# Small selection products fed with 112 rows, and a shorter step between attention and the first search

## The chip, the cores and the metric

The kernel runs on one core of one Trainium2 chip. The metric is the device time of one execution in microseconds (us), the median over runs. The core's engines are TensorE (PE in the profile, with its weight loads shown apart as PEld), VectorE (DVE), ScalarE (ACT) and GpSimd (POOL); SP is the queue that issues most transfers. Each engine works through its own instructions strictly in the order in which the program has them, and waits there for what another engine or a transfer has to deliver.

## The reference

Three layers one after the other, on 4 batches of 448 tokens, 12 heads of width 64 (1792 tokens, 768 features):

```python
scores = cap * np.tanh(scale * q @ k.T / cap)          # per batch and head
x = softmax(scores) @ v                                # -> 1792 x 768

logits = x @ w_gate                                    # first mixture: 8 experts
for idx in np.argsort(-logits.flatten()):              # best pair (token, expert) first
    if token_is_assigned or counts[e] >= N // E:       # each expert takes 224 tokens
        continue
    assigned[tok] = e
for e in range(8): out[mask_e] = relu(x[mask_e] @ w1[e]) @ w2[e]

y = relu(x @ w1[best]) @ w2[best] * gate               # second mixture: best expert of a token,
out = x + y                                            # where x @ w_skip > 0
```

The greedy assignment of the first mixture is what makes "searches" necessary: eight times over, the kernel finds which expert fills up next and which 224 tokens it gets.

## The kernel before

**Attention** (`attention_bounded`) works on 24 pairs of heads, in four steps for each pair, 96 steps in all. Step `n` runs the entries of the table `STEP` in order. `outs[j]` (tile `osb`) holds pair j's sums of values times probabilities, transposed, in one of 11 buffers; `sums[j]` holds the probabilities added over the parts of the keys, from which a TensorE product with ones makes the denominators. `evac` copies `outs` from PSUM. `rows1` turns a group's gate logits and denominators into rows, and `rows2` turns one pair's output into rows: four transposes on TensorE into one of two `tp` buffers, a scaling by the reciprocal (on VectorE inside the attention, as eight activations on ScalarE in the search), and one transfer into `out`. Pairs that are ready for `rows2` wait in the list `ready`; inside the attention one leaves it per four steps while it holds more than `HOLD` pairs.

**The tail** (`TAIL`) finishes pair 23: its value sums are copied, `small` makes its denominators and gate logits, `small_evac` copies those, `rows1` makes rows of them and `logits` adds them to the table `L`. For all other pairs VectorE has added up `sums`; for the last one it adds only the first two parts, and `small` multiplies the other two with ones on TensorE. `w` is one matmul whose result nobody uses, and `d` is a `rows2`.

**The first search** (`route`, p = 0) finds the first expert. It is a chain in which six digits of a threshold follow one another: VectorE compares (`r_ge`, L913), TensorE counts with 16 products (L926), VectorE tests, TensorE spreads the result over all partitions (L932). Code stops at each `yield`, a "hop"; hops 1 to 3 hold VectorE work alone, the digits begin with hop 4. `ROWS` says after which hops a `rows2` is put into the program, and what is left in `ready` comes behind the last hop. Then ranks (L970, L971) and the list of tokens follow (L986, and L994 for the token ids), the first rows are gathered, and the experts begin.

**Experts.** While the experts multiply (`mm3`: L723, L724, L725 for narrow groups, L720 and L725 for wide ones), the later searches run between the matmuls, one behind the other. A planner (`clk`, `hop`, `tick`) places its hops by fixed estimates. For p from 1 to 6 every digit ends in a product that spreads the count of passing experts, L944: the column `nok` of 8 rows, repeated 112 times, times `aboveI` (8x8). There are 36 of these. L994 makes token ids of a list, from 16 rows, two products for each of the eight lists. All 16 or 8 rows lie at partition 0.

Of the kernel before, what the change touches and what calls it, by code (L numbers as in the profile page):

```python
# [19 lines left out]
P = 112  # L20
# [7 lines left out]
def attn_moe_moe2(ctx: ExitStack, tc: tile.TileContext, q, k, v, cap, wg1, w1a, w2a, wskip, wg2, w1b, w2b, out):  # L28
# [132 lines left out]
    toid = consts.tile([16, 3], BF, name="toid")  # L161
    aboveb = consts.tile([64, P], BF, name="aboveb")
    aboveI = consts.tile([E, E], BF, name="aboveI")
# [44 lines left out]
    def constants5():  # L208
        nc.vector.tensor_tensor(eq8, identf[:16, :8], identf[:16, 8:16], op=OP.add)
        nc.vector.reduce_max(toid[:, 0:1], identf[:16, :8], axis=AX.X)  # L210
        nc.vector.reduce_max(toid[:, 1:2], identf[:16, 8:16], axis=AX.X)
        nc.vector.scalar_tensor_tensor(toid[:, 2:], toid[:, 0:1], 8.0, toid[:, 1:2], op0=OP.mult, op1=OP.add)
        nc.vector.tensor_scalar(aboveI, identf[:E, :E], ABOVE, None, op0=OP.mult)
        nc.gpsimd.memset(aboveb, ABOVE)
# [27 lines left out]
    def attention_bounded(begin, search):  # L242
# [10 lines left out]
        with tc.tile_pool(name="aw", bufs=2) as work, \  # L253
# [111 lines left out]
            def add(n):  # L365
# [36 lines left out]
            def small(j, ns):  # L402


                ps = lgt[j] = banks[j % 2]
                todo = [(slice(0, 128), sums[j][:, :1], sums[j][:, 1:])]
                todo += [(None if part(n) == 3 else slice(0, 128), prob[n][:, :1], prob[n][:, -1:]) for n in ns]
# [62 lines left out]
            HOLD = 6  # L470
# [6 lines left out]
            TAIL = 'w evac w d small sevac d w w w w rows1 logits'  # L477
            ROWS = (1, 2, 3, 5, 7, 9, 11, 13)
# [33 lines left out]
            for n in range(NS):  # L512
# [4 lines left out]
                for t in STEP:  # L517
# [16 lines left out]
                    if t == "add" and n < NS - 1:  # L534
                        add(n)
# [22 lines left out]
            steps = {"evac": lambda: evac(last, False), "small": lambda: small(last, left), "sevac": lambda: small_evac(last),  # L558
                     "rows1": lambda: (rows1([last], True), ready.append(last)), "logits": lambda: logits([last]),
                     "w": lambda: warm(1), "d": lambda: rows2(ready.pop(0)), "a": lambda: rows2(ready.pop(0), True)}  # L560
            left = [n for n in range(NS - 4, NS) if part(n) == 3 or n > [m for m in range(NS - 4, NS) if part(m) < 3][1]]
# [9 lines left out]
            while search(sum_tile):  # L571
                hops += 1
                if ready and hops in ROWS:
                    rows2(ready.pop(0), True)
            while ready:
                rows2(ready.pop(0), True)
# [65 lines left out]
    def experts_(ctx, attend):  # L642
# [202 lines left out]

        def begin():
            nc.gpsimd.memset(act, 1.0)
# [13 lines left out]
        def route():  # L861
# [23 lines left out]
            st = flat[:16, n2:n2 + T].rearrange("p (h a j) -> p h a j", h=2, j=8)  # L885
            for p in range(E):
# [14 lines left out]
                if p < E - 1:  # L901
# [4 lines left out]
                    for i, (sh, w) in enumerate(DIG):  # L906
# [27 lines left out]
                        else:  # L934
                            pc = rt([E, 64])
                            for c in range(NCH):
                                nc.tensor.matmul(pc[:, :B_], ohb[:, c, :], ge[:, c // 2, :B_, c % 2], start=(c == 0), stop=(c == NCH - 1))  # L937
                            ok = keep([E, 64], BF, "r_okt", bufs=2)
                            nok = keep([E, 1], BF, "r_nok", bufs=2)
                            nc.vector.tensor_scalar(ok[:, :B_], pc[:, :B_], float(CAP), None, op0=OP.is_ge, op1=OP.add,  # L940
                                                    accum_out=nok)
# [46 lines left out]
                nc.vector.tensor_tensor(st, bc(pl[:, :, :, None], [16, 2, P // 8, 8]), bc(eq8[:, None, None, :], [16, 2, P // 8, 8]),  # L988
# [497 lines left out]
```

## Time and profile before

| what | value |
|---|---|
| median of 3 runs (732.33 to 737.96) | 732.43 us |
| profiled execution, its own time | 734.41 us |
| its span, first to last instruction | 732.7 us |
| busy: PE, DVE, ACT, POOL | 681.3, 566.5, 429.5, 167.8 us |

The span falls into these stretches, by the busy time of the engines and the clock that TensorE was granted (1.00 is 2.4 GHz, 0.50 is 1.2 GHz):

| from, to (us) | what runs | PE busy | DVE busy | ACT busy | POOL busy | clock |
|---|---|---|---|---|---|---|
| 0 to 216.70 | attention | 212.10 | 171.96 | 185.07 | 34.55 | 1.00 |
| 216.70 to 224.85 | tail | 7.93 | 4.16 | 1.84 | 0.00 | 1.00 |
| 224.85 to 241.75 | first search | 11.42 | 9.24 | 14.85 | 0.00 | 0.63 |
| 241.75 to 255.60 | list, gather, first features | 9.78 | 6.40 | 2.12 | 4.88 | 0.71 |
| 255.60 to 490.00 | experts 0 to 4, with searches 1 to 7 | 220.30 | 197.74 | 95.41 | 77.00 | 0.98 |
| 490.00 to 732.70 | the other experts, second mixture | 219.79 | 177.00 | 130.21 | 51.41 | 0.96 |

A busy share says little about a single stretch: what counts is which engine the others wait for at its end.

### The profile page before, as it was taken

To read this page: it belongs to the slowest core of one execution; us is meant where nothing else is said; L and a number is where in the kernel's file an instruction comes from. 1 tells how busy PE (TensorE), PEld (TensorE's weight loads), DVE (VectorE), ACT (ScalarE), POOL (GpSimd) and SP (SyncE) were. 2 spreads that over 40 slices of the span, in tenths; PEclk is the share of its full clock that TensorE was granted. 3 is DMA by queue.
4 is the path that set the end of the run, shared out by engine and by line. 5 is a ranking of instruction groups with operands and counts; after the bars stand their busy time and mean duration, and the time that the engine had idled before them with its cause. 6 is when DMAs were issued, how large, how long until landed. Compare 5 with 4: busy or idle time off the path is not lost.

```text
span 732.7 us, 13921 instructions
## 1 busy us (share of the span) xinstructions
PE 681.3 (93%) x5085; PEld 530.3 (72%) x5085; DVE 566.5 (77%) x1456; ACT 429.5 (59%) x737; POOL 167.8 (23%) x207
## 2 busy tenths in 40 slices
PE   7999999999998699998999999999998999899991
PEld 4445454555445488796888887889997999889990
DVE  4888887878775489798888788797687777978781
ACT  4999898989866333342343442446663665457560
POOL 2121302111100233143332432341123021440301
PEclk9999999999997699999999999999999999999996
DMA  5543233444113755544474643748853684768701
GB/s 123 123 123 76 64 97 81 102 101 100 51 38 102 239 182 166 162 151 155 125 212 143 210 155 115 221 145 257 257 180 107 212 252 132 234 227 235 234 18 47
DMA packets 140825, 109.09 MB, mean 149 GB/s; under 512 B 53825, under 2 KB 137281, under 8 KB 140737
## 3 DMA queue, kind: packets, MB, share of 16 engines
q1 hardware_dynamic: 135408, 90.02, 41.8%
q0 software_dynamic: 4368, 17.76, 7.8%
q8 instruction: 44, 0.72, 0.4%
q14 instruction: 45, 0.36, 0.2%
q10 hardware_dynamic: 960, 0.23, 0.1%
HBM read 95.60 MB, written 13.07 MB: 148 GB/s over the span
## 4 chain that ended last, share of the span: by engine, by line
PE 67%; DVE 16%; issue 9%; DMA 3%; POOL 2%; ACT 1%; SPq 0%; POOLq 0%; DVEq 0%; ACTq 0%
PE mm L720 13%; PE mm L725 10%; PE o L363 8%; PE s L331 7%; PE mm L723 5%; PE mm L724 4%; DVE wl L697 4%; PE o L359 3%; PE rt L937 2%; PE tp L423 2%; DMA xg<-out_dram,idx 2%; PE tp L300 2%; PE s L327 2%; PE o L394 1%; PE tp L290 1%
## 5 line engine op out<-in xcount | busy, mean ns | idle before, releaser
L720 PE MATMUL mm<-h,wh 128*128 128x448 f32 x528 | 182.7, 395 | 3.4 <-DVE h L798 3.4
L690 ACT ACTIVATE wh<-raw 128x768 fp32r<-128x768 f32 (+1 forms) x158 | 145.4, 926 | 8.0 <-DMA raw<-in_moe_w_dram 8.0
L725 PE MATMUL mm<-h,wl 128*128 128x224 f32 x528 | 142.5, 270 | 2.2 <-DVE wl L697 1.5
L725 PE MATMUL mm<-x,wl 128*128 128x224 f32 x528 | 143.5, 272 | 0.7 <-DVE wl L697 0.7
L692 POOL TENSOR_TENSOR wl<-raw,wh 128x768 fp32r<-128x768 f32 (+1 forms) x33 | 72.5, 2198 | 199.6 <-ACT wh L690 167.8
L720 PEld LDWEIGHTS mm<-h,wh 128*128 128x128 f32 x528 | 102.1, 193 | 11.6 <-DVE h L798 3.9
L725 PEld LDWEIGHTS mm<-h,wl 128*128 128x128 f32 x528 | 103.7, 196 | 3.4 <-DVE wl L697 2.5
L725 PEld LDWEIGHTS mm<-x,wl 128*128 128x128 f32 x528 | 102.0, 193 | 1.1 <-DVE wl L697 1.1
L337 ACT ACTIVATE p<-s,sc 128x896 f32<-128x896 f32 x96 | 87.5, 913 | 16.4 <-PE s L331 14.5
L813 ACT ACTIVATE t<-mm 128x224 f32<-128x224 f32 x66 | 23.5, 356 | 120.8 <-PE mm L725 120.8
L723 PE MATMUL mm<-x,wh 128*128 128x224 f32 x312 | 94.0, 301 | 0.0
L697 DVE TENSOR_TENSOR wl<-raw,wh 128x256 fp32r<-128x256 f32 x199 | 91.1, 496 | 0.1
L340 ACT ACTIVATE p<-p,capc 128x896 f32<-128x896 f32 x96 | 90.4, 943 | 0.0
L703 DVE TENSOR_TENSOR wl<-raw,wh 128x768 fp32r<-128x768 f32 (+1 forms) x68 | 70.9, 1051 | 21.3 <-ACT wh L690 20.8
L724 PE MATMUL mm<-x,wh 128*128 128x224 f32 x312 | 86.7, 278 | 0.5 <-DVE x L771 0.5
L720 PE MATMUL mm<-x,wh 128*128 128x448 f32 x216 | 70.2, 381 | 0.0
L363 PE MATMUL o<-p,raw 128*64 128x448 f32 x288 | 69.8, 564 | 0.1
L331 PE MATMUL s<-sq,sk 64*128 64x448 f32 x432 | 64.7, 404 | 2.1 <-DVE sk L280 0.9
L797 ACT ACTIVATE h<-mm 128x224 fp32r<-128x224 f32 x52 | 18.6, 357 | 78.3 <-PE mm L725 77.4
L723 PEld LDWEIGHTS mm<-x,wh 128*128 128x128 f32 x312 | 60.1, 193 | 3.0 <-issue 1.1
L331 PEld LDWEIGHTS s<-sq,sk 64*128 64x128 f32 x432 | 36.0, 189 | 35.3 <-ACT p L337 13.4
L724 PEld LDWEIGHTS mm<-x,wh 128*128 128x128 f32 x312 | 60.5, 194 | 0.7 <-DVE x L771 0.7
(330 smaller groups left out, 1098.6 us busy)
## 6 DMA issues: line engine op xcount, KB each, us to landing
raw<-in_moe_w_dram SPq DMA_DIRECT2D x44, 768.0 KB, 4.9
raw<-in_moe_w_dram SPq DMA_DIRECT2D x32, 1024.0 KB, 5.5
raw<-in_q_dram SPq DMA_DIRECT2D x48, 112.0 KB, 2.9
out_dram<-xt SPq DMA_DIRECT2D x24, 224.0 KB, 2.7
raw<-in_v_dram SPq DMA_DIRECT2D x24, 192.0 KB, 2.6
raw<-in_k_dram SPq DMA_DIRECT2D x46, 96.0 KB, 2.8
raw<-in_moe_w_dram POOLq DMA_DIRECT2D x2, 768.0 KB, 7.8
raw<-in_moe_w_dram POOLq DMA_DIRECT2D x1, 1024.0 KB, 10.4
```

The source lines that it names most:

```text
L331: nc.tensor.matmul(ps[:, h, :S], kst[j][f, a, s], q[f, b], start=(m == 0), stop=(m == 2))
L337: nc.scalar.activation(prob[n], pps.pop(n)[:, :m, :S], AF.Tanh, scale=sc8)
L340: nc.scalar.activation(prob[n], prob[n], AF.Exp, scale=capc)
L363: nc.tensor.matmul(o[64 * h:64 * h + 64], v[:, s], p[:, h], start=(i == 0), stop=(i == 3), skip_group_check=True)
L690: nc.scalar.activation(wh[:, :k], src, AF.Copy)
L692: nc.gpsimd.tensor_tensor(wl[:, :k], src, wh[:, :k].bitcast(F32), op=OP.subtract)
L697: nc.vector.tensor_tensor(wl[:, a:b], src[:, a:b], wh[:, a:b].bitcast(F32), op=OP.subtract)
L703: nc.vector.tensor_tensor(wl[:, :k], src, wh[:, :k].bitcast(F32), op=OP.subtract)
L720: nc.tensor.matmul(ps.rearrange("p a t -> p (a t)"), wh[:, i, :], x[:, i].rearrange("p a t -> p (a t)"), start=first, stop=last, skip_grou ...
L723: nc.tensor.matmul(ps[:, 0], wh[:, i, :], x[:, i, 0], start=first, stop=False)
L724: nc.tensor.matmul(ps[:, 0], wh[:, i, :], x[:, i, 1], start=False, stop=False)
L725: nc.tensor.matmul(ps[:, 0], wl[:, i, :], x[:, i, 0], start=False, stop=last, skip_group_check=wide)
```

## The change

1. The two kinds of small products get 112 rows in place of 8 and 16. The added rows are zeros: `nok` becomes two fixed tiles of 112 rows and `oh` (where `st` lies) is cleared once, both by GpSimd in `begin`, in the middle of the attention; `toid` and `aboveI` are made 112 rows long, zero below.
2. VectorE adds all parts of the last pair into `sums`; `small` then has two products with ones in place of six.
3. `TAIL` loses both `d` and all but one `w`; `HOLD` goes from 6 to 3, so that three more pairs are written out inside the attention; `osb` has 8 buffers, not 11; the search writes out 8 pairs, two of them after hop 1, the last after hop 11; before it wrote out 9, the last two of them after hop 13 and behind the last hop.

```diff
-    toid = consts.tile([16, 3], BF, name="toid")
+    toid = consts.tile([P, 3], BF, name="toid")
-    aboveI = consts.tile([E, E], BF, name="aboveI")
+    aboveI = consts.tile([P, E], BF, name="aboveI")
...
-                if n == full[2] and j < NH // 2 - 1:
+                if n == full[2]:
                     ADD[1].tensor_tensor(s, s, prob[n], op=OP.add)
-                if n == max(full[1], xs[0]) and j < NH // 2 - 1:
+                if n == max(full[1], xs[0]):
...
-                outs[j] = work.tile([128, S], F32, name="osb", bufs=11)
+                outs[j] = work.tile([128, S], F32, name="osb", bufs=8)
...
-                for i, (k, *x) in enumerate(todo):
-                    for h in range(2):
-                        kk = k or slice(64 * h, 64 * h + 64)
-                        nc.tensor.matmul(ps[64 + 32 * h:96 + 32 * h], ones[kk], x[h][kk, 0], start=(i == 0), stop=(i == len(ns)),
-                                         skip_group_check=True)
+                for h in range(2):
+                    nc.tensor.matmul(ps[64 + 32 * h:96 + 32 * h], ones, sums[j][:, h], start=True, stop=True, skip_group_check=True)
...
-            HOLD = 6
+            HOLD = 3
...
-            TAIL = 'w evac w d small sevac d w w w w rows1 logits'
-            ROWS = (1, 2, 3, 5, 7, 9, 11, 13)
+            TAIL = 'evac small sevac w rows1 logits'
+            ROWS = (1, 1, 2, 3, 5, 7, 9, 11)
...
+            for t in noks:
+                nc.gpsimd.memset(t, 0.0)
+            nc.gpsimd.memset(oh, 0.0)
...
-            st = flat[:16, n2:n2 + T].rearrange("p (h a j) -> p h a j", h=2, j=8)
+            st = flat[:, n2:n2 + T].rearrange("p (h a j) -> p h a j", h=2, j=8)
...
-                            nok = keep([E, 1], BF, "r_nok", bufs=2)
+                            nok = noks[i % 2]
...
-                            nc.tensor.matmul(pn, bc(nok, [E, P]), aboveI, start=True, stop=True)
+                            nc.tensor.matmul(pn, bc(nok, [P, P]), aboveI, start=True, stop=True)
```

From the first expert on every engine's order is the same in both kernels. The first of the two places where it differs most is TensorE from the tail to the first digit; `lgs` are the gate logits and denominators, `thr` the unused matmul, `r_ge` the first digit's comparison. Before:

```order
L423 MATMUL tp<-identf,osb 112x128 x4
L411 MATMUL o_197<-sums,ones 32x448 x2
L411 MATMUL o_197<-p,ones 32x448 x4
L413 MATMUL o_197<-osb,raw_71 32x448
L423 MATMUL tp<-identf,osb 112x128 x4
L131 LDWEIGHTS thr
L131 MATMUL s<-thr 112x448
```

After (its L406, L407 and L417 are before's L411, L413 and L423):

```order
L417 MATMUL tp<-identf,lgs 112x96 x4
L406 MATMUL o_199<-sums,ones 32x448 x2
L407 MATMUL o_199<-osb,raw_71 32x448
L131 LDWEIGHTS thr
L131 MATMUL s<-thr 112x448
L417 MATMUL tp<-identf,lgs 112x128 x4
L417 MATMUL tp<-identf,osb 112x128 x16
L924 LDWEIGHTS r_ge_2557
```

Four products of `p` and both `rows2` of the tail are gone, and four `rows2` (16 transposes) now stand ahead of the first digit's count, where before there were three.

The other place is VectorE at the last pair's sums (`sums`, `p`), the split of its probabilities (`px`) and the last `rows2` of the attention (`xt`). Before:

```order
L372 TENSOR_TENSOR sums<-p 128x896
L348 CAST px<-p 128x448
L349 TENSOR_TENSOR px<-p,px 128x448
L450 TENSOR_TENSOR xt<-tp,rec 112x512
L433 RECIPROCAL rec<-tp 112x4x6
L435 TENSOR_TENSOR g<-tp,rec 112x4x48
```

After (L444 is before's L450, L427 its L433):

```order
L372 TENSOR_TENSOR sums<-p 128x896
L375 TENSOR_TENSOR sums<-sums,p 128x896
L348 CAST px<-p 128x448
L349 TENSOR_TENSOR px<-p,px 128x448
L444 TENSOR_TENSOR xt<-tp,rec 112x512
L379 TENSOR_TENSOR sums<-sums,p 64x448 x2
L427 RECIPROCAL rec<-tp 112x4x6
```

One addition now stands ahead of the split, and two behind the `xt` of a `rows2`.

## Rows read from the trace of the kernel before

**Rows 1.** Timeline of PE round one L944: start us, duration us, engine, line.

```profile
260.65 0.27 PE L725 MATMUL mm<-x,wl 128*128 128x224 f32 x1
260.85 0.21 PE L944 MATMUL rt<-aboveI,r_nok 8*112 8x8 bf16 x1
260.99 0.37 PE L723 MATMUL mm<-x,wh 128*128 128x224 f32 x1
261.19 0.28 PE L724 MATMUL mm<-x,wh 128*128 128x224 f32 x1
```

**Rows 2.** Timeline of PE round L970 and L971, two products of 112 rows.

```profile
279.51 0.27 PE L725 MATMUL mm<-x,wl 128*128 128x224 f32 x1
279.62 0.18 PE L970 MATMUL rt<-r_cum,onesb 112*112 112x32 bf16 x1
...
279.70 0.35 PE L723 MATMUL mm<-x,wh 128*128 128x224 f32 x1
279.89 0.28 PE L724 MATMUL mm<-x,wh 128*128 128x224 f32 x1
```

**Rows 3.** Timeline of PE, the id products of one list.

```profile
363.04 0.26 PE L994 MATMUL rt<-toid,oh 16*112 16x3 bf16 x2
```

**Rows 4.** The chain that ended last, first and last L944 on it: start, us.

```profile
260.92 0.15 PE rt L944
...
469.38 0.14 PE rt L944
```

**Rows 5.** Timeline of DVE, copies of `outs` of pairs 4, 5, 8 and 9.

```profile
57.44 0.61 DVE L384 COPY osb<-o 128x448 f32<-128x448 f32 x1
65.16 0.61 DVE L384 COPY osb<-o 128x448 f32<-128x448 f32 x1
...
91.09 0.61 DVE L384 COPY osb<-o 128x448 f32<-128x448 f32 x1
99.38 0.62 DVE L384 COPY osb<-o 128x448 f32<-128x448 f32 x1
```

**Rows 6.** Timeline of all engines, end of the attention and tail.

```profile
209.69 1.26 DVE L379 TENSOR_TENSOR sums<-sums,p 64x448 f32<-64x448 f32 x2
...
215.41 0.93 PE L394 MATMUL o<-sums,ones 128*32 128x448 f32 x6
...
216.96 0.69 DVE L450 TENSOR_TENSOR xt<-tp,rec 112x512 f32<-112x512 f32 x1 [2.01 <-PE tp L423]
...
221.11 0.94 PE L413 MATMUL o<-osb,raw 128*32 128x448 f32 x2
...
222.43 0.54 ACT L417 ACTIVATE lgs<-o 128x448 f32<-128x448 f32 x1 [4.32 <-PE o L413]
...
224.85 0.29 DVE L889 TENSOR_REDUCE r_m<-L 112x16 f32<-112x128 f32 x1
```

**Rows 7.** Timeline of all engines, the first search's beginning and its end.

```profile
225.72 3.62 ACT L448 ACTIVATE xt<-tp,rec 112x64 f32<-112x64 f32 x17
...
226.13 0.65 PE L423 MATMUL tp<-identf,osb 128*112 128x128 f32 x4 [1.00 <-ACT xt L448]
...
227.25 0.67 PE L926 MATMUL s<-r_ohb,r_ge 112*64 112x8 bf16 x16 [0.47 <-DVE r_ge L913]
...
239.95 0.23 DVE L966 TENSOR_TENSOR_SCAN r_cum<-onesb,r_aq 112x32 bf16<-112x32 bf16 x1
...
241.75 0.18 PE L970 MATMUL rt<-r_cum,onesb 112*112 112x32 bf16 x1 [1.88 <-ACT xt L448]
```

**Rows 8.** Windows: PE, PEld, DVE, ACT, POOL busy us (x instructions), clock, DMA share, GB/s.

```profile
224.85:241.75 16.90, 11.42 (x133) 8.92 (x132) 9.24 (x50) 14.85 (x70) 0.00 (x0) 0.63 0.42 119
...
255.60:490.00 234.40, 220.30 (x2078) 195.94 (x2077) 197.74 (x708) 95.41 (x172) 77.00 (x63) 0.98 0.52 164
```

**Rows 9.** Timeline of PE after a long wait of expert 1.

```profile
341.24 0.55 PE L937 MATMUL rt<-r_ge,r_ohb 112*8 112x32 bf16 x16 [2.89 <-DVE r_ge L913]
...
342.37 0.60 PE L720 MATMUL mm<-h,wh 128*128 128x448 f32 x1
...
345.17 0.41 PE L720 MATMUL mm<-h,wh 128*128 128x448 f32 x1
```

More of the change, by code (lines that the diff above doesn't have):

```diff
@@ L400, in gates_of, with small @@
                                      skip_group_check=True)
-            def small(j, ns):
+            def small(j):
                 ps = lgt[j] = banks[j % 2]
-                todo = [(slice(0, 128), sums[j][:, :1], sums[j][:, 1:])]
-                todo += [(None if part(n) == 3 else slice(0, 128), prob[n][:, :1], prob[n][:, -1:]) for n in ns]
-                for i, (k, *x) in enumerate(todo):
-                    for h in range(2):
-                        kk = k or slice(64 * h, 64 * h + 64)
-                        nc.tensor.matmul(ps[64 + 32 * h:96 + 32 * h], ones[kk], x[h][kk, 0], start=(i == 0), stop=(i == len(ns)),
-                                         skip_group_check=True)
+                for h in range(2):
+                    nc.tensor.matmul(ps[64 + 32 * h:96 + 32 * h], ones, sums[j][:, h], start=True, stop=True, skip_group_check=True)
                 nc.tensor.matmul(ps[:32], wgb[:, j % NP], outs[j], start=True, stop=True, skip_group_check=True)
@@ L533, in attention_bounded @@
                         split_p(n + SA)
-                    if t == "add" and n < NS - 1:
+                    if t == "add":
                         add(n)
@@ L557, in attention_bounded @@
                 events.pop((t, n))()
-            steps = {"evac": lambda: evac(last, False), "small": lambda: small(last, left), "sevac": lambda: small_evac(last),
+            steps = {"evac": lambda: evac(last, False), "small": lambda: small(last), "sevac": lambda: small_evac(last),
                      "rows1": lambda: (rows1([last], True), ready.append(last)), "logits": lambda: logits([last]),
                      "w": lambda: warm(1), "d": lambda: rows2(ready.pop(0)), "a": lambda: rows2(ready.pop(0), True)}
-            left = [n for n in range(NS - 4, NS) if part(n) == 3 or n > [m for m in range(NS - 4, NS) if part(m) < 3][1]]
             for t in TAIL.split():
@@ L572, in attention_bounded @@
                 hops += 1
-                if ready and hops in ROWS:
+                for _ in range(min(len(ready), ROWS.count(hops))):
                     rows2(ready.pop(0), True)
-            while ready:
-                rows2(ready.pop(0), True)
+            assert not ready
     def attention_any(begin, search):
@@ L844, in experts_ @@
         dma = keep([P, ND, NCH], I32, "dma")
+        noks = [keep([P, 1], BF, "r_nok%d" % i) for i in range(2)]
         def begin():
+            for t in noks:
+                nc.gpsimd.memset(t, 0.0)
+            nc.gpsimd.memset(oh, 0.0)
             nc.gpsimd.memset(act, 1.0)
@@ L938, in route @@
                             ok = keep([E, 64], BF, "r_okt", bufs=2)
-                            nok = keep([E, 1], BF, "r_nok", bufs=2)
+                            nok = noks[i % 2]
                             nc.vector.tensor_scalar(ok[:, :B_], pc[:, :B_], float(CAP), None, op0=OP.is_ge, op1=OP.add,
-                                                    accum_out=nok)
+                                                    accum_out=nok[:E])
                             yield 0.5, 0.3
                             pn = rt([P, E])
-                            nc.tensor.matmul(pn, bc(nok, [E, P]), aboveI, start=True, stop=True)
+                            nc.tensor.matmul(pn, bc(nok, [P, P]), aboveI, start=True, stop=True)
                             n = keep([P, 1], F32, "r_n", bufs=2)
```

8 lines of the change are left out of this document (4 added, 4 removed).

## The prediction

> **What bounds the kernel now.** I read the stretches first. In the longest one that the change touches, the experts with the later searches, TensorE is busy 220.3 of 234.4 us and VectorE 197.7 [rows 8]: TensorE leads, with only 14 us of idle time, and VectorE has 37. Then the chain that ended last, in the same stretch, for the small products themselves: 32 of the 36 L944 stand on it, the first and the last of these in [rows 4], and 6 of the 7 L994 pairs that fall there (one pair is the first search's, before 255.6). So what one of them takes of TensorE is on the path. Of the 32, 28 are reached along TensorE and 4 from VectorE. Last, the timeline of the stretch from the last attention step to the first expert, where every step waits for one before it and no engine is full: the first search takes 16.9 us, at a mean granted clock of 0.63 [rows 8].
>
> **The products of 112 rows.** In [rows 1] one product of 8 rows stands between an L725 and an L723; from L725 to the next L724, whose starts the product and the two transitions move, it is 260.65 to 261.19, 0.54 us. In [rows 2] two products of 112 rows and 112 columns stand in the same place: 279.51 to 279.89, 0.38 us, for one product more. So at least 0.16 is saved if the 8-row product becomes a 112-row one. From L970 to L723 it is 0.08 for the two, 0.04 each; one less gives 0.34, so 0.20 is saved. I take 0.20. The L994 pair, 16 rows [rows 3], has the same forms of transition ahead and behind, and I give it 0.20 too.
>
> On the path: 28 x 0.20 = 5.6 for the L944 reached along TensorE; 4 x 0.10 = 0.4 for those reached from VectorE, where only the transition behind the product can shrink; 6 x 0.20 = 1.2 for L994. Together 7.2. Not all of it stays: each stretch of TensorE on the chain ends where VectorE waits for a search value, and if TensorE gets there earlier, VectorE is soon the later one. VectorE's 37 us of idle time are spread over those places, five times what is to be saved, so I let four fifths through: **-5.8**. Ends: -7.2 if all goes through, 0 if the rows are not what makes the product dear.
>
> What [rows 1 and 2] show is a transition: 0.20 us from L725 to the 8-row product, 0.11 from L725 to the 112-row one. The Trainium skill, TensorEngine Tiling (Array Packing), Key Properties, says that changing the tiling mode drains TensorE; the two spacings agree. The page TensorE: Matmul & The Clock Gate, LDWEIGHTS (loading the stationary operand), speaks against the edit: a load takes as long for 32 rows as for 128, only columns count. By that alone the product gains nothing from fewer or more rows, and the sum would be without this term; it is the first rival below.
>
> The clearing of `oh` and `nok` is GpSimd's, in the middle of the attention, beside 34.55 us of its work in 216.7 (table of the stretches); I cost it at nothing. If GpSimd were late with its split of v behind it, a step would wait for at most that clearing.
>
> **Three more pairs inside the attention.** They come into the 6th, 12th and 13th group of four steps. [Rows 5] give the price: the 6th group has no `rows2` and takes 65.16 - 57.44 = 7.72; the 10th, the same kind of group, has one and takes 99.38 - 91.09 = 8.29. So 0.57 each, TensorE's transposes nearly in full, and three make **+1.7**. Their transfers go into SP's queue ahead of loads for a unit several groups later, which hides them; the 8 buffers of `osb` are each free two steps before they are written again, by the order of steps.
>
> **The tail.** Before, the search's first instruction L889 starts at 224.85 [rows 6]. After, VectorE's `xt` of the attention's last pair ends at 216.96 + 0.69 = 217.65, and the two additions that now stand behind it take 1.26 (as at 209.69): `sums` is whole at 218.91. The addition ahead of the split falls on a VectorE that has little to do there, idle 2.01 ahead of that `xt`, and I cost it at nothing; without that cover it would cost about what the two behind take, 1.26. Then two products with ones and the one for the gate, in three column groups, like the three of L394 that took 0.93 together: 219.85. From the copy `lgs` to L889 it was 224.85 - 222.43 = 2.42, and nothing in that changes: 222.3. The tail ends **-2.5** earlier. If the gate product ran behind the two instead of beside them, it would cost its 0.94 [rows 6] more, so the ends are -2.5 and -1.6.
>
> **The first search.** With T for the start of L889: ScalarE takes 3.62 / 17 x 8 = 1.70 per pair [rows 7]. Only two `tp` buffers exist, so the third pair's transposes waited for ScalarE and came at T + 1.28 (226.13); the first count at T + 2.40 (227.25) was hidden from it. Now a fourth pair stands ahead of the count. Its buffer comes free 1.70 later, at T + 2.98, its transposes take 0.65, and TensorE, in order, counts at T + 3.6: **+1.2**. At half clock the transposes and the count take nearly twice as long, which adds up to 0.8; the mean of 0.63 says that the clock is down for most of this search already, and with five unused matmuls gone it may be down from its start. I take +1.6, between +1.2 and +2.0. The later pairs come into gaps that VectorE's compares leave, as before.
>
> At the end the ranks' L970 waited 1.88 for ScalarE's last pair and began at 241.75, while its input L966 was done at 239.95 + 0.23 [rows 7]. No pair is left there now, so up to 241.75 - 240.25 = 1.5 goes: **-1.4**. What is late next is VectorE's chain of digits itself. The weights' first loads stand behind the same pair in SP's queue and get no later; what an earlier start of theirs does to the gather I don't price.
>
> **The sum.** +1.7 - 2.5 + 1.6 - 1.4 = -0.6 up to the first expert, -5.8 after it: -6.4. The profiled execution took 734.41 for a span of 732.7, 1.7 more outside it, and would come to 728.0. It is 2.0 above the median of the three runs, so I go from the median: 732.43 - 6.4 = 726.0. A change of 1%, 7.3 us, is about what a measurement of this kernel can tell from none.
>
> **Rivals.**
> 1. The rows don't matter: the 8-row product is dear for its place among wide matmuls of another type, or for its one broadcast column. For it: [rows 2] differ from [rows 1] in the moving width too. Against it: the spacing ahead of the product, 0.20 against 0.11, has passed before anything moves through it. The time is 732.43 - 0.6 = 731.8. Chance 0.12.
> 2. VectorE takes the saving: its compares and splits become the later part at most places, and only a quarter of the 7.2 is left. For it: VectorE is busy 84% of the stretch, and TensorE's longest wait there, 2.89, is for a compare [rows 9]. Then -1.8 - 0.6: 730.0. Chance 0.15.
> 3. Everything goes through, and the earlier end of output rows lets the first gather land earlier as well: -7.2, -0.6 and up to 1 more: 723.6. Chance 0.15.
> 4. Slower: the clock. After TensorE's wait of 2.89 the wide matmul takes 0.60 against 0.41 at 345.17 [rows 9], so from 341.7 to 345.2 the clock is at its lower level, and of those 3.4 us nearly half is lost, 1.6. A TensorE that reaches VectorE's values sooner waits longer; each further wait that brings the clock down costs 1.6. The gain of 6.4 is gone from four more on, and with nine in the seven searches it would be 732.43 - 6.4 + 14.4 = 740. What speaks against it: most waits there are far under 2.89. The page TensorE: Matmul & The Clock Gate, HAM oscillation, tells of a kernel that falls back to the lower clock at its gaps between matmuls; [rows 9] agree, and by that rule alone this rival would be likelier than I make it. Chance 0.06.
>
> **How the numbers follow.** The forecast, 726.0, has 0.52. Its own range is 723 to 729: the share that goes through from a half to all (3.6 to 7.2), the tail and the search by 0.9 and 0.4 either way. Cases 1 and 2 reach to 731.8, case 3 down to 722.5. The range 722 to 732 leaves out the slower case and a little at either end. Faster by over 1% is under 725.1: a third of the forecast's 0.52 and all of case 3, 0.33 to 0.36. Slower by over 1% is case 4 alone.
>
> **What would show it.** In the profile after: L725 to L942 (the new number of L944) at 0.11 and L725 to L724 round it at 0.34, not 0.54; attention's last copies 1.7 later; the search's first instruction 0.8 earlier; the first count 3.6 to 4.4 behind it, with transposes released by ScalarE just ahead; no wait of the ranks' product for ScalarE; about the same or a longer wait of TensorE for VectorE among the experts, and the granted clock there still 0.98. The forecast is wrong if the spacing stays at 0.54, if the experts' stretch shrinks by less than half of 7.2 though the spacing has shrunk, or if the clock there falls.

## The result and the profile after

The changed kernel takes 725.28 us (median of 4 runs, 723.87 to 725.78); the kernel before, beside it on the same chip, 733.2 (4 runs, 732.33 to 737.96). The ratio is 0.9876, interval 0.983 to 0.9921: it is faster, by 7.9 us between the medians, by 9.1 by the ratio, and by the interval at least 5.8. The forecast was 726.0, 6.4 less than before. The profiled execution took 725.78 for a span of 724.0; of before it was 734.41 and 732.7. The ratios here leave out runs more than 1.5% above their kernel's fastest, so they need not be the quotient of the medians.

First the products. The changed kernel's timeline of PE (start us, duration us, engine, line, operation), round one spreading product, which is now L942; L717 is what was L725:

```profile
274.45 0.28 PE L717 MATMUL mm<-x,wl 128*128 128x224 f32 x1
274.56 0.17 PE L942 MATMUL rt<-aboveI,r_nok 112*112 112x8 bf16 x1
274.60 0.35 PE L715 MATMUL mm<-x,wh 128*128 128x224 f32 x1
274.78 0.27 PE L716 MATMUL mm<-x,wh 128*128 128x224 f32 x1
```

From L717 to the product it is 0.11, from L717 to L716 0.33; in [rows 1] the same steps were 0.20 and 0.54. That holds for all of them: over the 20 products that stand among matmuls of this size and wait for nothing the median goes from 0.55 to 0.33, over the dozen among wide ones (448 columns) from 0.64 to 0.42. The pairs of id products, whose price was taken over by likeness, save the same: from L717 to L716 round a pair among the same matmuls it is 0.38 or 0.39, before it was 0.60. So 0.22 is saved at each, where the forecast had 0.20.

Second the tail. All engines at the end of the attention; these rows answer to [rows 6], and L406, L407, L411, L444 and L887 are what was L411, L413, L417, L450 and L889:

```profile
219.23 0.69 DVE L444 TENSOR_TENSOR xt<-tp,rec 112x512 f32<-112x512 f32 x1 [1.59 <-PE tp L417]
...
219.83 1.26 DVE L379 TENSOR_TENSOR sums<-sums,p 64x448 f32<-64x448 f32 x2
...
220.59 1.12 PE L406 MATMUL o<-sums,ones 128*32 128x448 f32 x3 [0.46 <-DVE sums L379]
...
221.16 0.56 PE L407 MATMUL o<-osb,raw 128*32 128x448 f32 x1
...
222.51 0.54 ACT L411 ACTIVATE lgs<-o 128x448 f32<-128x448 f32 x1 [2.13 <-PE o L407]
...
224.74 0.29 DVE L887 TENSOR_REDUCE r_m<-L 112x16 f32<-112x128 f32 x1
```

The two additions (1.26) stand behind `xt`, the gate product L407 runs beside the sums L406, and from `xt` to the search's first instruction it is 224.74 - 219.23 = 5.51, before 224.85 - 216.96 = 7.89: 2.38 saved.

Third the first search, the same view; these rows answer to [rows 7] (L442, L417, L924, L964 and L968 were L448, L423, L926, L966 and L970):

```profile
226.02 0.65 PE L417 MATMUL tp<-identf,osb 128*112 128x128 f32 x4 [1.00 <-ACT xt L442]
...
227.66 0.65 PE L417 MATMUL tp<-identf,osb 128*112 128x128 f32 x4 [0.99 <-ACT xt L442]
...
228.24 1.00 PE L924 MATMUL s<-r_ohb,r_ge 112*64 112x8 bf16 x16
...
240.98 0.22 DVE L964 TENSOR_TENSOR_SCAN r_cum<-onesb,r_aq 112x32 bf16<-112x32 bf16 x1
...
241.26 0.27 PE L968 MATMUL rt<-r_cum,onesb 112*112 112x32 bf16 x1 [1.40 <-DVE r_cum L964]
```

A fourth pair's transposes (227.66), released by ScalarE, stand right ahead of the first count, which is 3.50 behind the search's first instruction (before 2.40). It takes 1.00, before 0.67, since the clock fell at 228.3; in the second profile of this kernel it falls 5.5 behind the search's first instruction and not 3.6, and the count takes 0.67 there too. The ranks' product waits for VectorE's `r_cum`, and no longer for ScalarE.

Fourth the two long stretches, as windows (PE, PEld, DVE, ACT, POOL busy us with instructions, clock, DMA share, GB/s); they answer to [rows 8]:

```profile
224.74:241.26 16.52, 10.79 (x129) 8.44 (x128) 9.33 (x50) 13.00 (x63) 0.00 (x0) 0.61 0.39 112
253.60:478.23 224.63, 207.62 (x2067) 189.35 (x2068) 195.17 (x702) 94.98 (x172) 77.18 (x61) 0.99 0.55 172
```

The second window goes from the first expert matmul to the write of the eighth list's ids. Between the same two events before had 488.38 - 255.58 = 232.80 us, with TensorE busy 218.70. So the stretch is 8.2 us shorter, TensorE has 11.1 less to do in it, and it waits 2.9 more (17.0 against 14.1).

All kernels below are read by the same five events of their timelines, in us of their own span: the copy of `outs` of pair 22, the search's first instruction, the ranks' product, the first expert matmul, the eighth list's ids. The last column is the distance of the last two.

| kernel | pair 22 | search | ranks | experts | list 8 | experts to list 8 |
|---|---|---|---|---|---|---|
| before | 210.98 | 224.85 | 241.75 | 255.58 | 488.38 | 232.80 |
| after | 213.25 | 224.74 | 241.26 | 253.60 | 478.23 | 224.63 |
| after, second profile (after_again) | 212.72 | 224.23 | 240.42 | 253.71 | 480.05 | 226.34 |
| e1_products | 210.88 | 224.74 | 241.65 | 255.68 | 482.12 | 226.44 |
| e2_tail | 212.98 | 224.48 | 240.67 | 253.58 | 489.13 | 235.55 |
| e3_clear224 | 212.87 | 224.37 | 240.58 | 253.65 | 479.77 | 226.12 |
| e4_rows13 | 213.18 | 224.67 | 239.86 | 252.86 | 480.15 | 227.29 |
| e5_rowcount | 213.43 | 224.92 | 241.13 | 254.22 | 480.95 | 226.73 |
| e6_best | 212.93 | 224.43 | 239.88 | 252.91 | 477.54 | 224.63 |
| e7_best_warm | 213.81 | 225.29 | 240.62 | 254.03 | 477.09 | 223.06 |
| e8_weights_late | 213.77 | 225.26 | 241.74 | 254.05 | 475.40 | 221.35 |
| e9_weights_behind | 213.33 | 224.83 | 241.23 | 260.09 | 482.05 | 221.96 |
| e10_rows14 | 213.44 | 224.94 | 242.87 | 257.23 | 479.79 | 222.56 |

### The profile page after: what moved, and what is told of

It is laid out like the page before. It is cut to its first block, busy times and chain, and to the rows that moved or that the text cites. A ratio compares the mean times of both kernels' runs of the same rounds, so it can differ in the third digit from the quotient of the medians.

```text
span 724.0 us, 13895 instructions
## 1 busy us (share of the span) xinstructions
PE 667.9 (92%) x5072; PEld 524.4 (72%) x5072; DVE 568.0 (78%) x1460; ACT 427.6 (59%) x729; POOL 171.2 (24%) x210
## 4 chain that ended last, share of the span: by engine, by line
PE 66%; DVE 16%; issue 10%; DMA 3%; POOL 2%; ACT 1%; SPq 0%; POOLq 0%; DVEq 0%; ACTq 0%
PE mm L712 13%; PE mm L717 9%; PE o L363 8%; PE s L331 7%; PE mm L715 4%; PE mm L716 3%; DVE wl L689 3%; PE o L359 2%; PE tp L417 2%; DMA xg<-out_dram,idx 2%; PE rt L935 2%; PE tp L300 2%; PE s L327 2%; PE o L394 1%; PE tp L290 1%
## 5 line engine op out<-in xcount | busy, mean ns | idle before, releaser
L717 PE MATMUL mm<-h,wl 128*128 128x224 f32 x528 | 142.6, 270 | 3.9 <-DVE wl L689 2.0
L717 PE MATMUL mm<-x,wl 128*128 128x224 f32 x528 | 142.6, 270 | 0.5 <-DVE wl L689 0.5
L717 PEld LDWEIGHTS mm<-h,wl 128*128 128x128 f32 x528 | 103.7, 196 | 5.5 <-DVE wl L689 3.3
L717 PEld LDWEIGHTS mm<-x,wl 128*128 128x128 f32 x528 | 101.1, 191 | 0.7 <-DVE wl L689 0.7
L715 PE MATMUL mm<-x,wh 128*128 128x224 f32 x312 | 92.9, 298 | 0.0
L689 DVE TENSOR_TENSOR wl<-raw,wh 128x256 fp32r<-128x256 f32 x199 | 88.3, 482 | 0.1
L716 PE MATMUL mm<-x,wh 128*128 128x224 f32 x312 | 85.9, 275 | 0.3 <-DVE x L763 0.3
L716 PEld LDWEIGHTS mm<-x,wh 128*128 128x128 f32 x312 | 59.8, 192 | 0.5 <-DVE x L763 0.5
```

What stands on the lines that cost most here:

```text
L689: nc.vector.tensor_tensor(wl[:, a:b], src[:, a:b], wh[:, a:b].bitcast(F32), op=OP.subtract)
L715: nc.tensor.matmul(ps[:, 0], wh[:, i, :], x[:, i, 0], start=first, stop=False)
L716: nc.tensor.matmul(ps[:, 0], wh[:, i, :], x[:, i, 1], start=False, stop=False)
L717: nc.tensor.matmul(ps[:, 0], wl[:, i, :], x[:, i, 0], start=False, stop=last, skip_group_check=wide)
```

## The experiments

The theory is that of the prediction: the small products are dear because few rows divide TensorE's array in another way than the 128-row matmuls round them, and most of what they save stays. Its rivals are that the rows don't matter, that VectorE takes the saving, and that the gain comes from the tail and the earlier output rows.

**The two halves apart.** e1_products is the kernel before with the products and the clearing alone (cut to the main lines):

```diff
                             pn = rt([P, E])
-                            nc.tensor.matmul(pn, bc(nok, [E, P]), aboveI, start=True, stop=True)
+                            nc.tensor.matmul(pn, bc(nok, [P, P]), aboveI, start=True, stop=True)
...
+            nc.gpsimd.memset(oh, 0.0)
```

> The kernel before with the products of 112 rows and the clearing alone; attention, tail and first search as before. Theory (changing the array's rows costs, and most of it is on the path): 0.33 from the matmul ahead of the spreading product to the second one behind it, as after, against 0.55; the searches among the experts end 5 to 6 us sooner; the clearing costs 0.8 in the attention; the first expert begins 0.8 later than before: 733.2 - 5.5 + 0.8 = 728.5. Rival (the gain of the whole change came from the shorter start and from fewer spells at the lower clock): the spacing shrinks, but VectorE takes it: 732 to 733.

Measured: 728.36 (12 runs, 722.2 to 733.73) against 732.46 (23 runs), ratio 0.9917, 0.9888 to 0.9946: 6.1 us less, 4.0 to 8.2. e2_tail is the rest alone (cut to two lines of it):

```diff
-            TAIL = 'w evac w d small sevac d w w w w rows1 logits'
-            ROWS = (1, 2, 3, 5, 7, 9, 11, 13)
+            TAIL = 'evac small sevac w rows1 logits'
+            ROWS = (1, 1, 2, 3, 5, 7, 9, 11)
```

> The other half alone: tail, sums, output rows and 8 buffers as after, products of 8 and 16 rows, no clearing. Theory: attention 1.7 longer, tail 2.4 shorter, first count 1.1 later, no wait for ScalarE ahead of the ranks; the ranks begin about 1.3 sooner than before, and because output rows no longer stand ahead of the weights in the queue, the first expert's first matmul comes 2.8 sooner: 733.2 - 2.8 = 730.4. Rival (the early gather of the profile after was chance): the first matmul comes 1.3 sooner, 731.9.

Measured: 731.66 (12 runs, 727.21 to 735.98) against 732.46, ratio 0.9991, 0.9958 to 1.0025. The first expert matmul comes 2.0 sooner than before, where 2.8 was expected. The two windows of the expert stretch, e1_products first and then e2_tail:

```profile
255.68:482.12 226.44, 212.91 (x2069) 194.51 (x2068) 194.57 (x703) 95.27 (x172) 76.70 (x61) 0.96 0.53 168
```

```profile
253.58:489.13 235.55, 220.65 (x2067) 196.19 (x2066) 196.10 (x703) 95.16 (x172) 76.76 (x61) 0.96 0.51 163
```

With the products alone, TensorE's busy time falls from 218.70 to 212.91, by 5.8, and the stretch by 6.4, though the granted clock there is lower than before; with the tail alone the eighth list comes 0.75 later than before. The measured gain is the products'. The rest is no loss and no gain that these times can tell.

The profiles tell more if they are read from list to list (each time the write of a list's ids, as in the last event above). Each entry is the length in us, with the granted clock:

| lists | before | e2_tail | after | e9_weights_behind |
|---|---|---|---|---|
| 2 to 3 | 36.36, 1.00 | 36.75, 0.96 | 35.45, 1.00 | 35.43, 1.00 |
| 3 to 4 | 40.69, 0.96 | 41.43, 0.92 | 39.77, 0.96 | 37.00, 1.00 |
| 4 to 5 | 36.21, 1.00 | 36.22, 1.00 | 35.26, 1.00 | 35.69, 1.00 |
| 5 to 6 | 36.71, 1.00 | 36.72, 1.00 | 35.50, 1.00 | 35.49, 1.00 |
| 6 to 7 | 39.66, 0.96 | 41.50, 0.92 | 36.63, 1.00 | 36.64, 1.00 |
| 7 to 8 | 12.46, 1.00 | 12.45, 1.00 | 12.61, 1.00 | 12.60, 1.00 |

The first of these as windows, of before and of after:

```profile
286.29:322.65 36.36, 34.96 (x338) 30.79 (x336) 30.11 (x113) 14.05 (x27) 11.10 (x8) 1.00 0.48 152
```

```profile
283.01:318.46 35.45, 34.03 (x338) 30.46 (x337) 30.17 (x113) 14.18 (x28) 11.12 (x8) 1.00 0.51 158
```

Two things follow. An interval holds six spreading products and one pair of id products, 7 x 0.22 = 1.54 us of spacing saved. In the three intervals that have the full clock before and after (2 to 3, 4 to 5, 5 to 6) the saving is 0.91, 0.95 and 1.21: two thirds of it stay. And e2_tail, which is 2.23 ahead of before at its second list (284.06 against 286.29), falls back by 2.97 in just the three intervals in which its clock is lower than before's; in the other three both agree to 0.01. So the earlier start of the experts is passed on as far as the clock is the same, and this one profile lost it to the clock.

**How many rows it takes.** e5_rowcount gives the spreading products of one search different rows (the values of `nok` all stand in the first 8, the others are zero):

```diff
-                            nc.tensor.matmul(pn, bc(nok, [P, P]), aboveI, start=True, stop=True)
+                            rn = (16, 32, 64, 96, 112, 112)[i]
+                            nc.tensor.matmul(pn, bc(nok[:rn], [rn, P]), aboveI[:rn], start=True, stop=True)
```

> After, with the spreading product of the six digits fed with 16, 32, 64, 96, 112 and 112 rows (the other rows are zeros in every case, so the values are those of after). From the matmul ahead to the second one behind it, plain spacing being 0.22 among narrow matmuls. Theory (what costs is a change of how the array's rows are divided): 16 and 32 rows 0.55 as before's 8, 96 and 112 rows 0.33; 64 rows, the half, 0.55 too. Rival (the cost falls with the rows used): a step from each to the next, 64 rows about 0.45. Second rival (any number under 112 is dear): 96 rows 0.55.

Its timeline of PE, round a product of 64 rows and one of 96 (the spreading product is L943 here):

```profile
266.72 0.27 PE L717 MATMUL mm<-x,wl 128*128 128x224 f32 x1
266.93 0.21 PE L943 MATMUL rt<-aboveI,r_nok 64*112 64x8 bf16 x1
267.06 0.37 PE L715 MATMUL mm<-x,wh 128*128 128x224 f32 x1
267.27 0.27 PE L716 MATMUL mm<-x,wh 128*128 128x224 f32 x1
...
269.06 0.28 PE L717 MATMUL mm<-x,wl 128*128 128x224 f32 x1
269.18 0.17 PE L943 MATMUL rt<-aboveI,r_nok 96*112 96x8 bf16 x1
269.21 0.35 PE L715 MATMUL mm<-x,wh 128*128 128x224 f32 x1
269.40 0.27 PE L716 MATMUL mm<-x,wh 128*128 128x224 f32 x1
```

From L717 to L716 it is 0.55 with 64 rows and 0.34 with 96. The medians by rows: 16, 32 and 64 all have 0.55, 96 has 0.335 and 112 has 0.33. So it is a step between 64 and 96 rows, not a slope. Neighbours, type, columns and the one broadcast column are the same in all five, which leaves nothing of the rival by which the rows don't matter, nor of those by which the cost falls evenly or any number under 112 is dear. (One run, 726.53; its time tells nothing more.)

**The clearing.** GpSimd's clearing of `oh` was costed at nothing. e3_clear224 clears the 224 columns of each row that the id product reads, instead of 1792:

```diff
-            nc.gpsimd.memset(oh, 0.0)
+            nc.gpsimd.memset(oh.rearrange("p a c -> p (a c)")[:, NCH * (T // 8 + 24):NCH * (T // 8 + 24) + T], 0.0)
```

> After, with GpSimd clearing only the 224 columns of oh that st uses, not 1792. Theory (the long clearing holds VectorE's copy up, and through it TensorE): the copy that took 0.94 in the eighth group takes 0.39 again, that group loses its extra 0.8, and the time is 725.3 - 0.8 = 724.5. Rival (that group is longer for another reason, such as the first use of the eighth osb buffer): the group keeps its 0.8 and the time stays at 725.3.

Measured: 724.08 (6 runs), ratio 0.986, 0.9814 to 0.9905, not to be told from the change as it was. But the place shows it. After, all engines in the 8th group of four steps:

```profile
76.88 1.58 POOL L844 MEMSET oh<- 112x1792 bf16 x1
...
78.55 0.39 POOL L846 COPY avail<-desc 112x8 f32<-112x8 f32 x1
78.81 0.94 DVE L348 CAST px<-p 128x448 fp32r<-128x448 f32 x1
...
79.80 0.47 PE L359 MATMUL o<-px,vx 128*128 128x448 f32 x1 [1.00 <-DVE px L348]
```

and with the small clearing:

```profile
77.06 0.28 POOL L844 MEMSET oh<- 112x224 bf16 x1
...
79.00 0.39 DVE L348 CAST px<-p 128x448 fp32r<-128x448 f32 x1
79.44 0.68 PE L359 MATMUL o<-px,vx 128*128 128x448 f32 x2 [0.45 <-DVE px L348]
```

In these two VectorE's copy to `px` takes 0.94 where GpSimd's copy and clearings run beside it, and 0.39 where they are over; TensorE waits 1.00 for it, or 0.45, and in the kernel before 0.21. It isn't so in every execution. In after_again, the second profile of the changed kernel, the copy takes 0.39 at the same place, and GpSimd's next clearings are the ones that take longer:

```profile
78.85 0.39 DVE L348 CAST px<-p 128x448 fp32r<-128x448 f32 x1
78.92 0.36 POOL L848 MEMSET dsh<- 112x16 int32 x1
```

In the seven profiles that have the moved row and the long clearing this group is 0.50 to 1.01 longer than before (0.79 in after, 0.50 in after_again); in the four that have the moved row without it (e2_tail has no clearing; e3_clear224, e6_best and e7_best_warm have the small one) it is 0.24 to 0.30. In e1_products, which has the long clearing but not the moved row, the copy takes 0.39 and the group is no longer than before (+0.01, where its expectation had 0.8). So 0.24 to 0.30 goes with the moved row, and another 0.2 to 0.8, by the execution, with the long clearing that has become its neighbour.

**Where the rows of the first search go.** e4_rows13 gives its eight pairs the hops of the kernel before, one pair to a hop:

```diff
-            ROWS = (1, 1, 2, 3, 5, 7, 9, 11)
+            ROWS = (1, 2, 3, 5, 7, 9, 11, 13)
```

> After, with the output rows of the search after hops 1, 2, 3, 5, 7, 9, 11, 13, one per hop. Theory (the fourth pair ahead of the first count is what made it late; the last pair after hop 13 is done before the ranks need the bank): first count 2.4 behind the search's first instruction, not 3.5; ranks 1.1 sooner, the first matmul of the experts too: 725.3 - 1.1 = 724.2. Rival (the gather and the first weights came early only because the last output rows were written two digits before them): the ranks come 1.1 sooner, but the weights' load waits for the last rows again and the gather takes over 6 to land, 726.

Measured: 723.39 (6 runs), ratio 0.9859, 0.9816 to 0.9903. Its first count is 2.40 behind the search's first instruction again, and from there to the ranks it is 239.86 - 224.67 = 15.19 us, after 16.52. Part of these 1.33 is the clock, which falls 3.6 us behind the search's first instruction in after and 5.1 behind it here. Between profiles that are nearer in this it is 1.00 (after_again, where the clock falls after 5.5 and the ranks come after 16.19) and 1.07 (after against e6_best, which has the rows of e4_rows13, a fall after 3.1, and 15.45). So the second pair of the first hop costs 1.0 to 1.1, which is what the first count shows, and a pair at hop 13 brings no wait of the ranks. The first expert matmul comes only 0.74 sooner than after, since the gathers take 5.5 us to land, after 4.6: of the rival, the longer landing came, though not its 726. e10_rows14 puts the last one at hop 14 instead, `ROWS = (1, 1, 2, 3, 5, 7, 9, 14)`, to bring back the wait that the change took away.

> After, with the last output rows of the search moved from hop 11 to hop 14, where the kernel before had its last ones. Theory (the start is earlier because no output rows stand ahead of the ranks' bank and of the weights in SP's queue): the ranks wait for ScalarE again, 1 us or more, the weights are issued 1 to 2 later, the gather lands in over 5.5, and the first matmul of the experts comes 2 later than in after; time 727. Rival (the start of the first expert is set by the digits alone): under 0.5 later.

```profile
242.87 0.19 PE L968 MATMUL rt<-r_cum,onesb 112*112 112x32 bf16 x1 [1.71 <-ACT xt L442]
```

In this timeline the ranks' product waits for ScalarE again, and comes 242.87 - 224.94 = 17.93 behind the search's first instruction, 1.41 more than after and 1.74 more than after_again; the forecast had 1.4 for this. The first expert matmul comes 3.63 later than after, where 2 was expected. The time is 726.34 (5 runs), ratio 0.9908, 0.9865 to 0.9952.

**The gather and the weights.** After, the first expert matmul comes 1.98 sooner, though the ranks come only 0.49 sooner. The two gathers of the first list's rows land 4.6 us after their issue (median), before 6.4. e8_weights_late was to issue the two loads of weights on SP's queue behind the gather's:

```diff
-        hop_until(won, 0)
-        pump(2)
         hop_until(listed, 0)
         busy0(24)
         fetch_rows(0)
+        pump(2)
```

> After, with the first two loads of weights put behind the first gather in the program. Theory (the gather landed 2 us sooner after the change because the weights started 1.3 sooner and were less in its way): with the weights behind it the gather lands in 4.6 us or less, the first split waits for its weights instead, and the first expert begins 2 to 4 later. Rival (the gather came sooner because the output rows were written long before): its landing stays at 4.6 whatever the weights do.

It did not act: SP, with nothing else queued, issued them at 242.32, 0.58 behind the ranks, as after (241.84, also 0.58). So its 723.5 (4 runs, ratio 0.9847, 0.9801 to 0.9893) is one more time of the change itself. e9_weights_behind gives all five loads to GpSimd's queue, where they stand behind the gather, by leaving `pump(2)` out.

> After, with all five first loads of weights issued by GpSimd behind its two gathers, so that none is on its way when the gather starts (in the run before with the same aim the queue issued them at the same time as in after, so it told nothing). Theory (weights in the gather's way set its landing): the gather lands in under 4.4, the weights land 4 to 6 later than in after, and the first split, not the gather, ends the start last. Rival (output rows in the gather's way): landing stays at 4.4 to 4.8.

The gathers land after 4.4, hardly sooner than after, but the weights come late and the experts start at 260.09 (728.37, one run). In e10_rows14, with a late output row and the weights issued at 244.28, the gathers take 6.9. The issues of both stretches, e10_rows14 first and then after (median us from issue to landing):

```profile
raw<-in_moe_w_dram SPq DMA_DIRECT2D x2, 768.0 KB, 5.7
...
xg<-out_dram,idx_all POOLq DMA_INDIRECT x2, 6.9
```

```profile
raw<-in_moe_w_dram SPq DMA_DIRECT2D x2, 768.0 KB, 6.0
...
xg<-out_dram,idx_all POOLq DMA_INDIRECT x2, 4.6
```

So where the last output row and the weights come earlier, the gather lands 2 us sooner. In all profiles the landing goes with the time by which the weights are issued ahead of the first gather: 4.4 to 4.5 us ahead it lands after 4.5 to 4.7 (after, after_again, e2, e3, e5, e8), 4.1 ahead after 5.1 to 5.6 (e4, e6, e7), 3.5 to 3.6 ahead after 6.4 to 6.9 (before, e1, e10), and with the weights behind it after 4.4 (e9). The last output row, which lands 2.7 us after its issue (median), should by this estimate be over even in e10_rows14 (242.84 + 2.7 = 245.5; the gather is issued at 247.81). That speaks for the weights. It isn't shown, because the row was moved along with them in every kernel but e9_weights_behind.

**The best of these, and the clock.** e6_best has the small clearing and the rows of e4_rows13. e7_best_warm adds the five unused matmuls that the change took out of the tail, `TAIL = 'w evac w small sevac w w w w rows1 logits'`, to see if they hold the clock in the first search. after_again is the changed kernel, unaltered, on the same chip.

> After with both edits that were tried one by one: GpSimd clears 224 columns of oh, and the search's output rows come after hops 1, 2, 3, 5, 7, 9, 11, 13. Theory (the two are at different places and add up): the eighth group 0.4 shorter, the ranks 1.1 sooner and with them the first matmul of the experts: 1.3 to 1.6 less than after. Rival (the start is soon lost again in the experts): the first matmul comes sooner, and the time is that of after.

> The same with all the unused matmuls of the kernel before put back into the tail, six in place of one. Theory (they keep the clock up into the first search, but cost TensorE time only where it waits): the clock falls one or two us later, the first counts take 0.67 in place of 1.0, the ranks come 0.3 to 0.5 sooner. Rival (they stand in TensorE's order ahead of the last pair's sums and transposes): the search's first instruction comes 0.4 later and nothing is won.

> After once more, for a second profile of the same program and a narrower interval. Theory (executions of one program differ by the spells of TensorE's lower clock in the experts, 1.6 to 1.9 us for each that falls where TensorE leads): up to the first expert every time agrees within 0.4 with the first profile, and further on the two drift apart only across such spells. Rival (they differ all along, by transfers): the difference grows evenly.

| kernel | us | runs | ratio to before | interval |
|---|---|---|---|---|
| e6_best | 723.01 | 6 | 0.9846 | 0.9807 to 0.9885 |
| e7_best_warm | 724.35 | 6 | 0.9858 | 0.982 to 0.9896 |
| after_again | 724.68 | 6 | 0.9842 | 0.9799 to 0.9886 |

e6_best reaches its ranks 15.45 behind the search's first instruction, after_again 16.19, but no time here separates the three. With the unused matmuls the clock falls at 230.2 instead of 227.5, 4.9 behind the search's first instruction instead of 3.1; but the changed kernel alone shows 3.6 and 5.5 in its two profiles, so this isn't shown to be their doing. The ranks come 15.33 behind the first instruction instead of 15.45: nothing is won.

The expectation for after_again held in its second half. Up to the first expert the two profiles of one program differ by more than the 0.4 that it allowed, by 0.84 at the ranks: 0.29 of it arises in the group with the clearing, 0.33 in the first search, where the clock falls later, and the rest at the start. Among the experts they agree to 0.15 from list to list where both have the full clock, and differ by 0.49 and 0.81 from list 3 to 4 and from 6 to 7, where the clock differs.

One thing about the clock goes with how the experts begin. The first 12 us of the experts as windows, of before, e1_products, after and e6_best in this order:

```profile
255.58:267.58 12.00, 10.99 (x106) 9.73 (x104) 10.97 (x32) 5.26 (x11) 4.14 (x2) 0.86 0.66 217
```

```profile
255.68:267.68 12.00, 11.52 (x82) 10.72 (x81) 9.17 (x26) 4.79 (x9) 4.14 (x2) 0.57 0.65 215
```

```profile
253.60:265.60 12.00, 9.48 (x108) 8.60 (x109) 11.01 (x34) 5.72 (x11) 4.10 (x2) 1.00 0.78 262
```

```profile
252.91:264.91 12.00, 9.33 (x109) 8.46 (x108) 11.01 (x35) 5.68 (x11) 4.15 (x2) 1.00 0.70 235
```

Where TensorE waited 0.88 to 1.67 us for the gathered rows behind its unused matmuls (before 1.23, e1_products 1.67, e4_rows13 0.88, e10_rows14 1.40) the clock drops to its lower level at the start of the experts, to a mean of 0.57 to 0.86; in the eight profiles where it waited for the first of them 0.35 or not at all it is 1.00 throughout. In e9_weights_behind, where TensorE waited 6.79 a little later, the experts begin at the lower level too. With one short drop the stretch up to the second list costs little more (29.47 in e4_rows13, 29.56 in e6_best), since VectorE is busy 11.0 of the 12 us and sets the pace; with the long drop of e1_products it is 31.48.

## Why the prediction was right

The sign, the range and the main term held: 725.28 against 726.0. That the number came so near is in part luck: the attention cost more than was forecast, while the first search's fourth pair cost less and the gather gave a gain that was not priced. By its own steps:

- **The products, -5.8.** Right in mechanism and near in size. The spacing saved is 0.22 where 0.20 was taken, and the products alone save 6.1 us by their ratio (4.0 to 8.2) and 5.8 of TensorE's busy time. e5_rowcount shows that it is the rows. The Trainium skill, TensorEngine Tiling (Array Packing), Key Properties, has a change of tiling mode drain TensorE; the step between 64 and 96 rows agrees. No view here shows the drain itself. The share of four fifths was too high and the base too small, and the two errors cancel: six intervals between lists save 6 x 1.54 = 9.2 us of spacing, where the forecast counted 7.2 for the products on the chain, and two thirds of that stay by the three intervals at full clock, 6.1. What is lost shows as waits of TensorE, 17.0 us in the stretch after, 14.1 before.
- **Three more rows in the attention, +1.7.** Mis-sized. The 6th, 12th and 13th groups grew by 0.57, 0.57 and 0.58, as forecast. The 8th, for which nothing was forecast, grew by 0.79: about 0.25 with the moved row, the rest with the clearing costed at nothing (0.50 in all in the second profile). Together 2.5, of which 2.27 shows at pair 22, since this profile reaches the attention's pairs 0.27 sooner from the start.
- **The tail, -2.5.** Right: 2.38, with the gate product beside the sums. (The row of L394 that it was likened to holds six products, not three; the time came out all the same.) With the longer attention, the search begins 0.1 sooner and not 0.8, in the second profile 0.6.
- **The fourth pair, +1.6.** Right in mechanism, mis-sized. The fourth pair's transposes and the first count came 2.92 and 3.50 behind the search's first instruction, forecast 2.98 and 3.6 at full clock: 1.10 later than before, and e4_rows13 prices the pair at 1.0 to 1.1 over the whole search. The addition for half clock did not come, as the clock was still full while these transposes ran (0.65). Nor is it "nearly twice": at the lower level four transposes take 1.10 for 0.65 and a count 1.02 for 0.67. **The ranks' wait, -1.4**, went as said, and e10_rows14 brings it back at 1.4 to 1.7. The ranks come 0.49 sooner than before, in the second profile 1.33, forecast 0.6.
- **Gather and weights, not priced.** They gave another 1.5: the experts start 1.98 sooner. In the profiles this start is passed on where the clock is the same. e2_tail loses its own only where its clock is lower; e9_weights_behind, whose experts start 6.5 later than after's, has its second list 6.19 later, and comes within 3.8 at the eighth because after's clock is lower from list 3 to 4 (39.77 against 37.00). The time of e2_tail, 3.1 less to 1.8 more, holds the whole 2.0 and nothing.
- **The clock.** The rival that feared it did not come: the granted clock of the expert stretch is 0.99 after and 0.98 before. Single profiles of kernels with the new products go from 0.95 to 1.00 there, but over all runs on record the mean clock of a whole execution is 0.960 to 0.964 before, by the group of runs, and 0.962 to 0.967 with them. Three stretches of it in before (from 256.5, 341.5, as in [rows 9], and 444) run the same matmuls in 0.41 for 0.27 or 0.60 for 0.41; the first profile of after has one, from 337.5. That accounts for some 2 us of the 8.2 by which its stretch is shorter: from list 6 to 7, where only before has one, 3.03 are saved, elsewhere some 1. It is not the change's doing: the second profile of the same kernel has three, and a stretch shorter by 6.5.
- **VectorE takes the saving** (730.0). Refuted by the ratio of e1_products, whose interval ends at 4.0 us less; 1.8 would be a quarter. VectorE's `r_ge` is waited for 6.8 us in five places after, 5.9 in four before: the waits grow, as said, but little.

What stays open: the halves, 6.1 and 0.7 by their ratios, make 6.8, and the whole, as it was timed with its near copies, 0.984 to 0.988, some 9 to 12. The intervals are wide enough to meet. Read from the profiles at equal clock the halves make more, 6.1 from the lists and 2.0 from the start. Part may be the clock at the start of the experts, which is full only where the early gather is, and which in e1_products cost 1.9 us (31.48 against 29.56); this was read from single profiles and not tried by itself.

## What to carry to other kernels

A small matmul between large ones costs what it does to its neighbours, so read the spacing from the matmul ahead to the second one behind, not its own duration; if its rows are few and the others have 128, filling it up with zero rows can be worth more than the rows cost. An edit on an idle engine is not free if it can hold up the engine beside it: look at what it will stand beside after all other edits, not at its place before. And compare two profiles stretch by stretch, where both have the same clock, before you call a gain lost or won: two profiles of one program differed here by 1.8 us at the eighth list.

## What had not been expected of the hardware

- The cost of a product of few rows is a step: 0.55 us of spacing for 16, 32 and 64 rows, 0.33 for 96 and 112.
- VectorE's copy of 128x448 took 0.93 to 1.22 instead of 0.39 beside GpSimd's work; in e1_products and after_again it took 0.39 and GpSimd's clearings of 112x16 beside it up to 0.36 instead of 0.11. The Trainium skill, SBUF — State Buffer, Who interferes with whom, has GpSimd and a VectorE instruction in a two-port mode hold a shared port pair in turn, whoever issues first. That one of the two is held up agrees; the mode of this copy, and which was issued first, no row shows.
- An indirect gather of 112 rows took 4.4 to 6.9 us from issue to landing, longer the shorter before it the weights were issued.
- A wait of TensorE of 0.88 to 1.67 us, behind unused matmuls, went with a drop of the clock at the start of the next stretch in four profiles of four; one of 0.35 did not.
